# Denominator rows broadcast from 32 source rows instead of 8, with a new instruction order and one relu free to choose its engine

## The chip, the cores and the metric

The kernel runs on one core of one Trainium2 chip. The time is the device time of a run in microseconds (us). Each version is run several times and the runs in the fast state are compared. All comparisons use fast runs alone; two slow runs of the kernel before (552.36 and 390.58 us) are left out of them. TensorE's clock was granted in full (0.998 to 1.000) in every trace that this text reads. The experiments ran in four groups (1 to 4, 5 to 8, 9 to 11, and 12) on four chips, each beside the kernel before, whose medians there were 268.31, 268.89, 268.65 and 269.29 us; so a ratio is compared first with those of its own group.

## The reference, cut to what matters

Four layers follow one another over x of 1 x 2048 x 512 bf16 values: linear attention with 32 heads of 16 columns, a feed-forward block of 1376 hidden units, and both once more with the same weights.

```python
def _A_ref(x, wqkv, wo):                     # attention without softmax
    ...                                      # q, k, v by head
    phi = lambda t: jnp.where(t > 0, t + 1, jnp.exp(t)) + 1e-6
    pq, pk = phi(q), phi(k)
    kv  = jnp.einsum("bhsd,bhse->bhde", pk, v)
    z   = jnp.einsum("bhsd->bhd", pk)
    num = jnp.einsum("bhqd,bhde->bhqe", pq, kv)
    den = jnp.einsum("bhqd,bhd->bhq", pq, z)[..., None] + 1e-6
    o = num / den                            # one denominator per head and row
    return o.transpose(0, 2, 1, 3).reshape(B, S, D) @ wo

def _B_ref(x, w1, w2):
    return jnp.maximum(x @ w1, 0) @ w2       # written with einsum there

x = x + _A_ref(_layernorm(x), A_wqkv, A_wo)
x = x + _B_ref(_layernorm(x), B_w1, B_w2)
... # the same two lines once more
```

## The kernel before

Every operation is put on a list with what it reads and writes. Two text tables then fix the whole schedule: ORDER gives the place of each operation in the instruction streams and, for those that may run on either engine, a letter (`a` ScalarE, `d` VectorE); BANKS gives the PSUM bank of each tile. Both come from an offline search.

The denominators of a chunk of 512 rows go this way: a matmul with the mask Zc, logarithm and exponential on ScalarE (which makes 1/den), a write to DRAM, and four broadcasts that bring each head's row to the 16 partitions of that head. VectorE then multiplies.

```python
mm_group(... Zc[:, j, :] ..., name="den%d" % t)     # 32 columns per group of 8 heads: 4 copies of each head
g.add(ACT, ... ACTF.Ln ...)
g.add(ACT, ... ACTF.Exp, scale=-1.0 ...)            # rsp = 1/den
r = rdram[cur_layer[0] // 2, t]
dma(lambda e: e.dma_start(r, rsp[:, s, :]), ...)
for j in range(4):
    i = 4 * t + j
    dma(lambda e, i=i, j=j: e.dma_start(xn[:, i, :],
            r[32 * j:32 * j + 8, :].unsqueeze(1).broadcast_to([8, 16, 512])), ...)   # 8 rows, each 16 times
...
# a_den_mul: VectorE, L855
e.tensor_tensor(unit_ap(us[j]), unit_ap(us[j]), xn[:, i, :], ALU.mult)
```

After an attention block the residual is added, the row is centred into `xn`, and one DMA transposes two row tiles of `xn` into `Tb`, from which the next matmuls read. It is issued from the same queue as the broadcasts.

```python
# resid_a
g.add_flex([(ACT, ... activation(xn[:, i, :], xres[:, i, :], ACTF.Identity, bias=nmf ...)),
            (DVE, ... tensor_scalar(xn[:, i, :], xres[:, i, :], nmf ..., ALU.add))], ..., name="cen%d" % i)
# tr_dma, L484
dma(lambda e: e.dma_start_transpose(Tb[:, lo:hi, ...], xn[:, lo:hi, ...]), ...)
```

The feed-forward block uses products of seven multiplications for eight. Its fourth output block is summed by `hadd` and gets its relu from `hq`, on VectorE only:

```python
g.add(DVE, ... tensor_tensor(out_ap(1, 1), pv(X), s6 ..., ALU.add), name="hadd%d_%d" % (t, js[0]))
g.add(DVE, ... tensor_scalar(out_ap(1, 1), out_ap(1, 1), 0.0, None, ALU.max), name="hq%d_%d" % (t, js[0]))
```

Two groups of matmuls do no work and keep TensorE busy at the start; some experiments change their number:

```python
for ... in range(WARM): last = e.matmul(psv[:, wt, :], wrm[:, 0:128], wrm[:, :], ...)           # WARM = 10
... [(psv[:, wt, :], wrm[:, 0:128], wrm[:, :], True, True, False)] * NFILL                      # NFILL = 2
```

## Time and profile before

| | before |
|---|---|
| time, median of 3 runs | 268.69 us (the two fast ones are 268.33 and 268.69) |
| span in the profile | 267.4 us |
| TensorE busy | 260.0 us |
| VectorE busy | 240.7 us |
| ScalarE busy | 202.4 us |
| TensorE stalls between head and tail | about 2.6 us as the prediction counts them (2.4 corrected, see the end) |

The table is read from the bottom up. An engine that is 97% busy leaves little to gain, and the last line says how much: it is the sum of the gaps between matmuls, worked out with its lines in the prediction below.

### The profile page before, as it was taken

To read this page: it belongs to the slowest core of one execution; us is meant where nothing else is said; L and a number is where in the kernel's file an instruction comes from. 1 tells how busy PE (TensorE), PEld (TensorE's weight loads), DVE (VectorE), ACT (ScalarE), POOL (GpSimd) and SP (SyncE) were. 2 spreads that over 40 slices of the span, in tenths; PEclk is the share of its full clock that TensorE was granted. 3 is DMA by queue.
4 is the path that set the end of the run, shared out by engine and by line. 5 is a ranking of instruction groups with operands and counts; after the bars stand their busy time and mean duration, and the time that the engine had idled before them with its cause. 6 is when DMAs were issued, how large, how long until landed. Compare 5 with 4: busy or idle time off the path is not lost.

```text
span 267.4 us, 5269 instructions
## 1 busy us (share of the span) xinstructions
PE 260.0 (97%) x1919; PEld 171.5 (64%) x1937; DVE 240.7 (90%) x660; ACT 202.4 (76%) x446; POOL 19.6 (7%) x30
## 2 busy tenths in 40 slices
PE   7999999998999999999999999999999999999995
PEld 2444444546447888887875654454786778888883
DVE  4999999999789999999998998499989999889975
ACT  3999965889888786487788998799999869745320
POOL 4021000000030002201011000000000000130000
PEclk9999999999999999999999999999999999999999
DMA  6954882346234061401403400322592245201104
GB/s 209 382 115 82 195 306 71 127 78 162 38 107 91 0 81 21 82 0 22 77 13 69 78 2 2 103 93 43 131 175 50 39 42 99 81 0 22 80 2 157
DMA packets 47626, 23.61 MB, mean 88 GB/s; under 512 B 37008, under 2 KB 46192, under 8 KB 47600
## 3 DMA queue, kind: packets, MB, share of 16 engines
q1 hardware_dynamic: 47456, 23.24, 35.3%
q8 instruction: 15, 0.25, 0.4%
q14 instruction: 11, 0.09, 0.1%
q10 hardware_dynamic: 144, 0.03, 0.1%
HBM read 11.21 MB, written 3.15 MB: 54 GB/s over the span
## 4 chain that ended last, share of the span: by engine, by line
PE 85%; DVE 7%; DMA 5%; issue 1%; ACT 1%; SPq 0%; DVEq 0%
PE ps L538 84%; DMA Tb<-xn 3%; DMA xin<-in_A_x_dram 1%; DVE xres L551 1%; DVE xres L582 1%; DVE ps L1035 1%; DVE xn L970 1%; DVE xin L1061 1%; DVE xn L558 0%; ACT big L518 0%; PE ps L501 0%; DVE xn L578 0%; DVE bst L445 0%; DVE KVT L649 0%; ACT xn L556 0%
## 5 line engine op out<-in xcount | busy, mean ns | idle before, releaser
L520 ACT ACTIVATE escr<-ps 128x512 bf16<-128x512 f32 x56 | 33.3, 614 | 7.1 <-PE ps L538 7.0
L1021 ACT ACTIVATE big<-ps 128x512 bf16<-128x512 f32 (+1 forms) x57 | 29.2, 530 | 8.0 <-PE ps L538 7.7
L545 ACT ACTIVATE sqscr<-xres 128x512 bf16<-128x512 f32 x48 | 30.4, 633 | 5.3 <-DVE xres L582 2.6
L518 ACT ACTIVATE big<-ps 128x512 bf16<-128x512 f32 x56 | 33.3, 611 | 1.4 <-PE ps L538 1.3
L538 PE MATMUL ps<-big,xn 128*128 128x512 bf16 x122 | 30.2, 379 | 0.3
L538 PE MATMUL ps<-Tb,wqkv 128*128 128x512 bf16 x128 | 30.5, 379 | 0.0
L538 PE MATMUL ps<-gw,big 128*128 128x512 bf16 x121 | 29.2, 379 | 0.3
L538 PE MATMUL ps<-wqkv,Tb 128*128 128x512 bf16 x92 | 22.7, 379 | 0.7 <-ACT Tb L508 0.3
L524 DVE TENSOR_TENSOR big<-big,escr 128x512 bf16<-128x512 bf16 x56 | 22.4, 420 | 0.8 <-ACT big L518 0.2
L538 PE MATMUL ps<-w2s,big 128*128 128x256 f16 x160 | 21.9, 272 | 0.1
L538 PE MATMUL ps<-xn,w 128*128 128x256 f16 x140 | 21.8, 273 | 0.0
L538 PE MATMUL ps<-xn,xin 128*128 128x256 f16 x140 | 21.4, 273 | 0.2 <-DVE xn L970 0.2
L538 PE MATMUL ps<-w,big 128*128 128x256 f16 (+3 forms) x114 | 21.6, 301 | 0.0
L538 PEld LDWEIGHTS ps<-Tb,wqkv 128*128 128x128 bf16 x128 | 12.2, 98 | 14.3 <-issue 0.2
L538 PE MATMUL ps<-Tb,wper 128*128 128x256 bf16 x140 | 21.3, 272 | 0.0
L538 PEld LDWEIGHTS ps<-gw,big 128*128 128x128 bf16 x128 | 12.4, 98 | 12.7 <-issue 0.5
L538 PEld LDWEIGHTS ps<-big,xn 128*128 128x128 bf16 x128 | 12.0, 97 | 13.1 <-issue 0.7
L571 POOL TENSOR_TENSOR rstdf<-varf,nhalf 128x4 f32<-128x4 f32 x8 | 9.6, 1201 | 145.1 <-DVE varf L569 145.1
L538 PE MATMUL ps<-w,xin 128*128 128x256 bf16 (+2 forms) x145 | 19.7, 269 | 0.1
L1004 ACT ACTIVATE ps<-ps 128x512 f32<-128x512 f32 (+1 forms) x32 | 16.5, 514 | 4.4 <-PE ps L538 2.4
L1104 ACT ACTIVATE ps<-ps 128x256 f32<-128x256 f32 x27 | 10.0, 371 | 11.8 <-PE ps L538 10.3
L522 DVE TENSOR_SCALAR escr<-escr 128x512 bf16<-128x512 bf16 x56 | 15.6, 288 | 2.4 <-ACT escr L520 2.4
(160 smaller groups left out, 544.8 us busy)
## 6 DMA issues: line engine op xcount, KB each, us to landing
xn<-rdram SPq DMA_DIRECT2D x32, 128.0 KB
wqkv<-in_A_wqkv_dram SPq DMA_DIRECT2D x3, 512.0 KB, 7.1
xin<-in_A_x_dram SPq DMA_DIRECT2D x3, 512.0 KB, 7.9
out_dram<-xn SPq DMA_DIRECT2D x3, 512.0 KB, 2.6
w<-in_B_w_dram SPq DMA_DIRECT2D x1, 1376.0 KB, 6.9
w<-in_B_w_dram SPq DMA_DIRECT2D x1, 1280.0 KB, 9.9
rdram<-rsp SPq DMA_DIRECT2D x8, 128.0 KB, 1.7
wo<-in_A_wo_dram SPq DMA_DIRECT2D x1, 512.0 KB, 10.1
```

Of the source, the lines that this page charges most:

```text
L518: g.add(ACT, lambda e: e.activation(dst_ap, psv[:, b, :], ACTF.Identity, bias=1.0 + 1e-6, scale=1.0), [("ps", b)], [dst_key], C_ACT_PSUM, ...
L520: g.add(ACT, lambda e: e.activation(escr[:, s, :], psv[:, b, :], ACTF.Exp), [("ps", b)], [("escr", s)], C_ACT_EXP, name=name + "_exp")
L522: g.add(DVE, lambda e: e.tensor_scalar(escr[:, s, :], escr[:, s, :], 1.0, 1e-6, ALU.min, ALU.add), [("escr", s)], [("escr", s)], C_DVE_BF4 ...
L524: g.add(DVE, lambda e: e.tensor_tensor(dst_ap, dst_ap, escr[:, s, :], ALU.max), [dst_key, ("escr", s)], [dst_key], 340.0, name=name + "_phi")
L538: last = e.matmul(o, l, r, start=st, stop=sp, skip_group_check=skip)
L545: g.add(ACT, lambda e: e.activation(sqscr[:, q, :], xres[:, i, :], ACTF.Square, accum_out=dst[:, i:i + 1]), [("xres", i)], [("sqscr", q), ...
L551: g.add(DVE, lambda e: e.scalar_tensor_tensor(xres[:, i, :], psv[:, b, :], 0.0, src, ALU.add, ALU.add, accum_out=s1f[:, i:i + 1]), [("ps", ...
L571: g.add(POOL, lambda e: e.tensor_tensor(rstdf[:, sl], varf[:, sl], nhalf[:, 0:4], ALU.pow), [("varf", t), ("nhalf",)], [("rstdf", t)], C_P ...
L582: g.add(DVE, lambda e: e.scalar_tensor_tensor(xres[:, i, :], psv[:, b, :], rstdf[:, i:i + 1], xres[:, i, :], ALU.mult, ALU.add, accum_out= ...
L1004: g.add_flex([(ACT, lambda e: e.activation(dst(), psv[:, src, 0:W], ACTF.Identity), cost(C_ACT_PSUM)), (DVE, lambda e: e.tensor_copy(dst() ...
L1021: g.add_flex([(ACT, lambda e: e.activation(out_ap(r, m), pv(b), ACTF.Relu), cost(C_ACT_PSUM)), (DVE, lambda e: e.tensor_scalar(out_ap(r, m ...
L1104: g.add_flex([(ACT, lambda e: e.activation(psv[:, c1, cols], psv[:, c2, L], ACTF.Identity), 290.0), (DVE, lambda e: e.tensor_copy(psv[:, c ...
```

## The change

The intent: a broadcast that reads 32 rows can be spread over all 16 DMA rings, one that reads 8 only over 8 (a ring is here the share of a transfer that one of the core's 16 DMA engines moves; each reports its end by a semaphore update of its own); a relu that may run on either engine relieves VectorE; and with these new costs the order is searched again.

```diff
-ORDER, BANKS   (old tables; 63 and 3 lines)
+ORDER, BANKS   (new tables; 11 operations go from ScalarE to VectorE, 8 the other way, about 100 matmul groups move)
-        esel, ehead = ...                      # never read
-        def den_consts(): ...                  # filled them
-   affine_select(zm1[:], onesf[:, 0:32], [[0, 4], [-16, 8]], ...)
+   affine_select(zm1[:], onesf[:, 0:32], [[-16, 8], [0, 4]], ...)
-   affine_select(zmask[:], zm1[:], [[0, 4], [16, 8]], ...)
+   affine_select(zmask[:], zm1[:], [[16, 8], [0, 4]], ...)
-   dma_start(xn[:, i, :], r[32 * j:32 * j + 8, :].unsqueeze(1).broadcast_to([8, 16, 512]))     # cost 650
+   dma_start(xn[:, i, :], r[32 * j:32 * j + 32, :].unsqueeze(1).broadcast_to([32, 4, 512]))    # cost 550
-   g.add(DVE, tensor_scalar(... ALU.max), name="hq...")
+   g.add_flex([(DVE, tensor_scalar(... ALU.max)), (ACT, activation(... ACTF.Relu))], name="hq...")
```

The mask edit puts the four copies of a head side by side, so that 32 consecutive rows each read 4 times give the same 128 rows as 8 rows each read 16 times. One of the moves is of the centring of row tile 2 in the first attention block (`cen2`), from ScalarE to VectorE.

> **What bounds the kernel now.** I read the engine totals first, then the chain that ended last, then who waited for whom, and only then the queues.
>
> ```profile
> PE 260.0 (97%) x1919; PEld 171.5 (64%) x1937; DVE 240.7 (90%) x660; ACT 202.4 (76%) x446; POOL 19.6 (7%) x30
> ...
> PE 85%; DVE 7%; DMA 5%; issue 1%; ACT 1%; SPq 0%; DVEq 0%
> PE ps L538 84%; DMA Tb<-xn 3%; DMA xin<-in_A_x_dram 1%; DVE xres L551 1%; DVE xres L582 1%; DVE ps L1035 1%; DVE xn L970 1%; DVE xin L1061 1%; DVE xn L558 0%; ACT big L518 0%; PE ps L501 0%; DVE xn L578 0%; DVE bst L445 0%; DVE KVT L649 0%;
> ```
>
> TensorE is the bound: busy 97%, 85% of the chain, clock 1.0 throughout. The change's title speaks of a full VectorE (90%), but a full VectorE costs time only where a matmul waits for it. Busy is not proof, since matmul ends are modelled, so I also took the start-to-start distances of the 1919 matmuls: the median is 216 ns for 512 columns and 109 ns for 256, and nearly all sit on the median. Some 16 gaps are one matmul too long with no waiter; those are missing records (1937 weight loads against 1919 matmuls), not stalls.
>
> The idle 7.4 us (267.4 - 260.0) splits into 1.24 before the first matmul, about 3.1 after the last (it starts at 264.25), and 3.2 of gaps, of which 0.8 belongs to the first layer norm, before 9 us. Of the rest one gap stands out. The chain in order of time shows it, and later stretches without a break:
>
> ```profile
> 61.63 4.97 DMA Tb<-xn
> 66.60 0.05 issue
> 66.65 7.31 PE ps L538 x38
> ...
> 194.44 4.37 DMA Tb<-xn
> 198.81 0.03 issue
> 198.83 0.43 DVE xn L970
> 199.27 0.05 issue
> 199.32 4.42 PE ps L538 x48
> ...
> 217.80 46.18 PE ps L538 x426
> ```
>
> At 66.65 TensorE waits for a transpose (L484) of 4.97 us; in the last feed-forward block it then works 46 us without an entry for anything else. The list of waits agrees:
>
> ```profile
> PE ps L538 <- DMA Tb<-xn: 1.0, 1, 1.0
> ...
> DVE xn L970 <- DMA Tb<-xn: 0.9, 1, 0.9
> ```
>
> Counted as start-to-start excess, the avoidable stalls after the head are 1.21 us at 66.65, 0.36 at 199.32, 0.31 at 176.56 (the KVT step), 0.31 at 102.97 and about 0.4 of crumbs: **2.6 us in all, 1.0% of the run**. No rescheduling that leaves the matmuls alone can win more between the head and the tail.
>
> **What the Trainium skill says.** "DMA: Bandwidth & Descriptors", section "Why a DMA increments its semaphore by 16 and not by 1": a transfer uses the largest k up to 16 that divides the slowest dimension of both sides, and the sequencer posts 16 - k at once. The old broadcast has 8 source rows, hence k = 8. The trace agrees: all 32 broadcasts show 9 semaphore updates (one early jump, then 8), everything else 16, and the page therefore gives no landing time for them:
>
> ```profile
> xn<-rdram SPq DMA_DIRECT2D x32, 128.0 KB
> ...
> Tb<-xn SPq DMA_TRANSPOSE x30, 3.2
> ...
> big<-hrt SPq DMA_TRANSPOSE x8, 2.5
> ```
>
> "TensorE: Matmul & The Clock Gate", "Wait — 56ns, not 53.3ns?", gives N/2.4 GHz plus about 2.5 ns for a warm matmul, 215.7 ns for 512 columns; the trace has 216, so these matmuls cannot run closer. "ScalarE: Activation LUTs", "What ACT_TABLE_LOAD costs", gives 186 ns + 0.833 ns per column for an ACTIVATE with immediate operands: 613 and 399 ns for 512 and 256 columns. The trace has 596 and 387 for L1021, the same relu out of PSUM.
>
> **The change, part by part.**
>
> *Broadcasts.* The columns of the denominator are reordered so that each head's four copies are adjacent; a broadcast then reads 32 rows 4 times instead of 8 rows 16 times. Bytes stay 128 KB, in 128 packets of 1 KB of 46 ns each (median of the trace). Per ring that is 16 x 46 = 0.74 us now and 8 x 46 = 0.37 us afterwards. The queue issues one every 0.62 us (0.58 plus a gap), so today a group of four gains a backlog of about 0.12 us per transfer, and afterwards none. From the semaphores a broadcast takes 2.6 to 2.8 us from issue to landing when alone and first, 3.1 to 3.4 at the end of a group, 3.7 to 4.4 behind a transpose. I estimate 2.3 us afterwards for each: rows arrive 0.4 us earlier at the front of a group, 0.9 us at its end. But the multiplication that consumes them (L855, 32 x 418 ns) shows no wait at all today, so this gain is hidden. What remains is what queues behind: the transpose at 194.44 (4.37 us, normally 3.1) and the hidden-unit transposes at 65.48 (3.7) and 198.25 (4.2), normally 2.4. The first gates the 0.36 us stall at 199.32. Its gain is up to 0.3 us, less because the new order puts one broadcast (0.6 us of issue) ahead of that transpose.
>
> *The 66.65 stall is not the broadcasts'.* The late transpose lands on 15 of 16 rings by 65.06 and on the last at 66.60. A 16 KB instruction fetch occupies one ring from 64.51 to 65.43, an 8 KB one from 65.15. At 140.13 there is the same picture with no broadcast near: fetch at 142.87, 15 rings at 143.30, the last at 144.93. So wider broadcasts do not cure it; a shifted schedule may move the transpose off the fetch, or another transpose onto one. I give it about even odds: 0.6 us expected of 1.2.
>
> *relu of the fourth block.* I compared the order texts: only 4 of 21 go to ScalarE, all in the last block, three of 256 columns and one of 512. VectorE loses 3 x 0.220 + 0.285 = 0.95 us, ScalarE gains 3 x 0.40 + 0.61 = 1.8 us. This lies in 204 to 264 us, where ScalarE is the emptier engine and TensorE has an unbroken 46 us: worth next to nothing.
>
> *Dead constants.* ehead and esel (0.199 + 0.220 us of VectorE near 41 and 44 us) go. TensorE is not waiting there: under 0.1 us.
>
> *The new order.* Eleven flexible evacuations move from ScalarE to VectorE and eight the other way, with some hundred matmul groups reordered, mostly in the last block. VectorE's total should stay within 1 us of 240.7. TensorE's work is identical.
>
> Sum: -0.6 (fetch collision, even odds), -0.2 (199), -0.2 for the smaller stalls that a new search should have tidied, -0.1 (constants), +0.2 for stalls that a new order makes: **-0.9 us, 268.69 to 267.8 us**.
>
> **The rivals.** (1) *Broadcasts are the bottleneck of the attention blocks*, and earlier rows pull everything forward by about 1 us per group. For it: the two long transposes in the chain stand next to broadcast groups. Against: no wait at L855, and the fetch explains the larger. It would give about 266.5, still capped by the 2.6 us. (2) *VectorE is the real bound*, as the title says, and relief of it pays. For it: 90% busy, and most small TensorE waits name VectorE. Against: those add up to little over 1 us, and the other moves hand VectorE more than half of the relief back. At most 1 us. (3) *The new order is worse on the chip than in the search that made it*: one tile needed too early stalls TensorE by 0.5 to 2 us, or a transpose meets an instruction fetch at a tight spot; with reordered groups in every block, 269 to 270 is possible.
>
> **Range and chances.** The floor is 268.7 - 2.6 = 266.1; two undisturbed runs of before differ by 0.36 us. So 266.5 to 269.3. Faster by 2% needs 263.3, below that floor; slower by 2% needs 274.1, that is 5 us of new stalls. Within 2%: 97%.
>
> **What would show it.** The broadcasts get a landing time on the page, near 2.3 us; TensorE's busy time stays within 2 us of 260; VectorE's within 1 us of 240.7; the hidden-unit transposes behind broadcasts fall to 2.4 to 3 us; the wait for a transpose near 66 us goes or stays with the instruction fetch's timing and not with the broadcasts. I would be wrong if TensorE had stalls that its records hide, if the spread of the rings slowed the transposes (all 16 rings shared, where 8 were free), or if the head or tail moved: their 9 and 3 us are outside my 2.6.

## The result, and the profile after

The kernel after takes 266.88 us (median of 4 runs, 266.66 to 267.25) against 268.85 us (median of 4 runs of the kernel before, the two of the table and the slow one among them). The ratio is 0.9935, with a 95% interval of 0.9914 to 0.9956: 0.65% faster, or 1.75 us (the fast runs' means are 268.67 and 266.92), which counts as the same at 2%. A ratio here is the record's, of the fast runs of the same rounds; it lies near the ratio of the means and is not quite that of the medians. A later set of six runs gave 0.9938 (0.9924 to 0.9951).

The profile page of the kernel after, engine totals, the chain that ended last by engine, and the landing time of the broadcasts (count, size of one, median us from issue to landing):

```profile
PE 258.9 (98%) x1919; PEld 172.3 (65%) x1937; DVE 240.3 (91%) x657; ACT 202.0 (76%) x447; POOL 18.7 (7%) x30
...
PE 92%; DVE 3%; DMA 2%; issue 1%; SPq 0%; DVEq 0%
...
xn<-rdram SPq DMA_DIRECT2D x32, 128.0 KB, 2.6
```

The busy times of all engines moved by about 1 us or less. What fell is the chain's share of other things than matmuls: TensorE's is 92% instead of 85%, and the transposes' 3% is gone from it. The broadcasts have a landing time now, 2.6 us, where the page had none.

The chain of waits of the kernel after, in order of time (start us, length us, what), around the place where the kernel before lost most, and in the last block:

```profile
54.89 17.90 PE ps L536 x124
72.79 0.05 issue
72.84 7.54 PE ps L536 x51
80.39 0.05 issue
...
185.65 0.16 issue
185.81 14.61 PE ps L536 x145
...
215.36 46.33 PE ps L536 x426
```

L536 is the matmul line, L538 before. From 54.89 to 72.79 us TensorE runs without a break, straight through the place where the transpose of 4.97 us stood; and from 185.81 to 200.42 through the one where that of 4.37 us stood. The list of waits (engine, what it wrote and its line, what it waited for: us in all, times, longest) has no entry of TensorE for a transpose any more; these are its largest entry for transposes (the other, L960, is 0.2 us) and the one for broadcast rows:

```profile
DVE big L702 <- DMA Tb<-xn: 1.2, 2, 0.8
...
DVE big L845 <- DMA xn<-rdram: 0.4, 1, 0.4
```

L845 is the multiplication that was L855. It had no wait before and has one now, of 0.4 us.

To place the gain, I cut the TensorE work at two matmuls that both kernels have: the third denominator of the first attention block (start at 56.47 us before) and the first of the second block (165.94 us), and compared start times. The head up to 56 us became shorter by 0.35 us, the first half by 1.49 and the second half, up to the last matmul, by 0.45: together 2.29, the difference of the spans 267.4 and 265.1. Over all versions measured below the head scatters from -0.5 to +0.2 us, once +1.84, with no link to the edits that I could find; so I count it as scatter and explain the other two.

**First half.** 1.21 us are the stall at 66.65, and 0.31 the one at 102.97; both are gone. **Second half.** 0.36 us are the stall at 199.32, gone too.

What happened at 66 us is read from the semaphore updates of the one transpose, which come ring by ring. In the kernel before: issued at 61.63, fifteen rings done at 65.06, the sixteenth at 66.60 (latency 4.97). After: 60.89, 64.07, 64.30 (3.40). In both an instruction fetch of TensorE's program, one packet of 16 KB, falls into this time: 64.51 to 65.43 before, 63.60 to 64.53 after. The DMA view of the kernel after, 61 to 68 us, has it (q8: packets, MB, share) beside the transpose that landed in time (median us to landing); experiment 9 shows the same view of the kernel before:

```profile
q8 instruction: 1, 0.02, 0.8%
...
Tb<-xn SPq DMA_TRANSPOSE x1, 3.4
```

The prediction put the late ring down to that fetch, and gave even odds that a new order would avoid it. The experiments had to decide between the fetch and the broadcasts.

### The profile page after: what moved, and what is told of

Same layout as the page of the kernel before. It is cut to its first block, busy times and chain, and to the rows that moved or that the text cites. A ratio compares the mean times of both kernels' runs of the same rounds, so it can differ in the third digit from the quotient of the medians.

```text
span 265.1 us, 5275 instructions
## 1 busy us (share of the span) xinstructions
PE 258.9 (98%) x1919; PEld 172.3 (65%) x1937; DVE 240.3 (91%) x657; ACT 202.0 (76%) x447; POOL 18.7 (7%) x30
## 3 DMA queue, kind: packets, MB, share of 16 engines
HBM read 11.21 MB, written 3.15 MB: 54 GB/s over the span
## 4 chain that ended last, share of the span: by engine, by line
PE 92%; DVE 3%; DMA 2%; issue 1%; SPq 0%; DVEq 0%
PE ps L536 92%; DMA wqkv<-in_A_wqkv_dram 2%; DVE bst L443 1%; DVE big L522 0%; DVE escr L520 0%; DVE xn L475 0%; DVE xn L576 0%; DVE Tb L507 0%; SPq L379 0%; SPq L381 0%; DVE KVT L647 0%; DVE xn L1166 0%; DVE mv L444 0%; DVEq L1389 0%; PE ps L499 0%
## 5 line engine op out<-in xcount | busy, mean ns | idle before, releaser
L536 PE MATMUL ps<-Tb,wqkv 128*128 128x512 bf16 x128 | 30.8, 379 | 0.0
L536 PE MATMUL ps<-big,xn 128*128 128x512 bf16 x122 | 30.1, 379 | 0.3
L536 PE MATMUL ps<-gw,big 128*128 128x512 bf16 x121 | 29.2, 379 | 0.5 <-issue 0.2
L536 PE MATMUL ps<-wqkv,Tb 128*128 128x512 bf16 x92 | 22.5, 379 | 1.0 <-DMA wqkv<-in_A_wqkv_dram 0.5
L536 PE MATMUL ps<-w2s,big 128*128 128x256 f16 x160 | 21.7, 273 | 0.0
L536 PE MATMUL ps<-xn,w 128*128 128x256 f16 x140 | 21.7, 273 | 0.0
L536 PE MATMUL ps<-xn,xin 128*128 128x256 f16 x140 | 21.5, 273 | 0.0
L536 PE MATMUL ps<-w,big 128*128 128x256 f16 (+2 forms) x114 | 21.4, 301 | 0.0
L536 PEld LDWEIGHTS ps<-Tb,wqkv 128*128 128x128 bf16 x128 | 12.1, 98 | 14.0 <-issue 0.2
L536 PE MATMUL ps<-Tb,wper 128*128 128x256 bf16 x140 | 20.8, 273 | 0.0
L536 PEld LDWEIGHTS ps<-gw,big 128*128 128x128 bf16 x128 | 12.3, 98 | 12.5 <-issue 0.5
L536 PEld LDWEIGHTS ps<-big,xn 128*128 128x128 bf16 x128 | 12.0, 98 | 13.0 <-issue 0.7
L536 PE MATMUL ps<-w,xin 128*128 128x256 bf16 (+2 forms) x145 | 19.6, 269 | 0.0
L569 POOL TENSOR_TENSOR rstdf<-varf,nhalf 128x4 f32<-128x4 f32 x8 | 8.5, 1065 | 143.5 <-DVE varf L567 143.5
L536 PEld LDWEIGHTS ps<-w2s,big 128*128 128x128 bf16 x160 | 15.2, 98 | 3.7 <-DVE xres L1090 0.9
```

The costliest lines, as they stand in the source:

```text
L536: last = e.matmul(o, l, r, start=st, stop=sp, skip_group_check=skip)
L569: g.add(POOL, lambda e: e.tensor_tensor(rstdf[:, sl], varf[:, sl], nhalf[:, 0:4], ALU.pow), [("varf", t), ("nhalf",)], [("rstdf", t)], C_P ...
```

## The experiments

**Theory A** (that of the prediction): the stall at 66 us belongs to the fetch, the new order moved the transpose to where the fetch doesn't hold it, and the broadcasts are worth about 0.2 us elsewhere. **Rival B:** the wide broadcasts free the queue, and the order is nothing but their consequence. **Rival C:** VectorE is the bound, and the relus on ScalarE are what paid.

### 1. Wide broadcasts alone, in the old order

```diff
 # the kernel before, with the two mask lines and
-   r[32 * j:32 * j + 8, :].unsqueeze(1).broadcast_to([8, 16, 512])
+   r[32 * j:32 * j + 32, :].unsqueeze(1).broadcast_to([32, 4, 512])
```

> The kernel before with the wide broadcasts alone (mask columns reordered, 32 rows read 4 times), its own order and relus. My theory (the broadcasts are hidden, the stall near 66 us comes from an instruction fetch on one ring): ratio 0.997 to 1.000, the broadcasts land in about 2.4 us, the stall near 66.6 us is still there with over 0.8 us, only the 0.36 us near 199 us shrinks. Rival 1 (the broadcasts delay the transposes): the stall near 66 us goes, ratio 0.993 to 0.995, the whole gain.

Measured: 268.61 us against 268.31, ratio 1.0004 (0.9987 to 1.0020): nothing. The chain of this kernel at the same place:

```profile
61.41 0.36 ACT big L518
61.77 4.95 DMA Tb<-xn
66.72 0.05 issue
66.76 7.31 PE ps L538 x38
```

The transpose is as late as before (its last ring at 66.72, the other fifteen at 65.19), with wide broadcasts in place: the stall is 1.20 us. So rival B falls for this stall. The second half is 0.45 us shorter than before, though, exactly what the kernel after has; the transpose near 194 us fell from 4.37 to under 3.5 us. This part is the broadcasts' own. Why the unprofiled runs do not show these 0.45 us isn't settled; the interval reaches to 0.9987, that is 0.35 us.

### 2. The new order with the old broadcasts

```diff
 # the kernel after, with the two old mask lines and
-   r[32 * j:32 * j + 32, :].unsqueeze(1).broadcast_to([32, 4, 512])
+   r[32 * j:32 * j + 8, :].unsqueeze(1).broadcast_to([8, 16, 512])
```

> The changed kernel with the old narrow broadcasts (8 rows read 16 times, old mask), the new order and the four relus on ScalarE kept. My theory (the order makes the gain): ratio 0.992 to 0.995 to the kernel before, no transpose stall near 65 us, a wait of up to 0.4 us may come back near 197 us. Rival 1: 0.997 to 1.000, stall back.

Measured: 269.25 us, ratio 1.0034 (1.0015 to 1.0052). This is slower than before, and a clear miss: theory A had the order carry most of the gain, and expected 0.992 to 0.995. The list of waits, and the chain near 66 us, of this kernel:

```profile
DVE big L845 <- DMA xn<-rdram: 3.6, 5, 1.8
```

```profile
63.69 4.39 DMA xn<-rdram
68.08 0.02 issue
68.10 0.04 DVE big L845
68.14 0.31 issue
68.44 0.69 DVE ps L995
```

VectorE now waits 5 times, 3.6 us in all, for broadcast rows, where the kernel before has no such wait and the kernel after one of 0.4 us. The search had been told that a broadcast costs 550 instead of 650 and placed the multiplications earlier. The transpose is issued at 61.75 instead of 60.89, and here all its rings are late (66.39), so that TensorE stalls there for 0.91 us again; and the second half, where the kernel after gains 0.45 us, loses 0.69. In the second half the rows are the cause that the trace shows: VectorE waits 0.30 and 0.84 us for them near 179 and 180 us, with no fetch on their broadcasts, and TensorE then waits for VectorE (0.74 us at 187.93). At 66 us the trace does not show this: no broadcast was queued ahead of that transpose, and a fetch (64.04 to 64.97) fell on it and on the broadcasts behind it, so broadcasts and fetch are not separated there. So order and broadcasts cannot be added up: the new order needs the rows early, in the second half at least.

### 3. The new order with all relus of the fourth block on VectorE

```diff
 # the kernel after, four entries of ORDER
-1301a ... 1427a ... 1443a ... 1533a
+1301d ... 1427d ... 1443d ... 1533d
```

> The changed kernel with the four relus of the fourth block back on VectorE. My theory (TensorE works unbroken there): equal to the changed kernel, ratio 0.9925 to 0.9950 to the kernel before, no new stall of over 0.2 us after 205 us. Rival 2 (VectorE is the bound there): 0.5 us or more is lost, ratio over 0.996.

Measured: 266.74 us, ratio 0.9939 (0.9924 to 0.9954), the same as the kernel after. The busy times of 56 us of the last block (stretch, length, then TensorE, weight loads, VectorE, ScalarE and GpSimd with their instruction counts, clock, DMA share, GB/s), first of the kernel after, then of this one:

```profile
204.00:260.00 56.00, 55.89 (x495) 45.95 (x495) 50.85 (x118) 33.37 (x77) 3.99 (x4) 1.00 0.18 48
```

```profile
204.00:260.00 56.00, 55.90 (x494) 45.90 (x495) 51.38 (x122) 31.88 (x73) 4.00 (x4) 1.00 0.18 48
```

VectorE has four instructions more and TensorE is as full as it was. Even here, where the relus are, VectorE is no bound: rival C falls.

### 4. The instruction fetch moved, first try

TensorE's program has 3,888 instructions, and one fetch packet appears for about every 256 of them. More instructions early therefore bring a later fetch forward in time. Here the idle matmuls at the start are cut into more and narrower ones, with about the same number of columns in all (10 x 512 = 5,120 and 31 x 165 = 5,115); with the weight loads that is 42 instructions more.

```diff
 # the kernel before
-WARM=10 ... e.matmul(psv[:, wt, :],     wrm[:, 0:128], wrm[:, :], ...)
+WARM=31 ... e.matmul(psv[:, wt, 0:165], wrm[:, 0:128], wrm[:, 0:165], ...)
```

> The kernel before with 31 warm-up matmuls of 165 columns in place of 10 of 512: the same warm-up time, 42 more TensorE instructions, so each of TensorE's instruction fetches comes some 42 instructions (about 4 us near 60 us) earlier. Nothing else differs. My theory: the fetch moves from 64.5 to about 60.6 us, the transpose issued at 61.6 us lands by 65.2 instead of 66.6 us, the 1.2 us stall goes, ratio 0.995 to 0.996. If the broadcasts make the stall, it stays and the ratio is 1.000.

Measured: 268.75 us, ratio 1.0015 (0.9992 to 1.0039). The fetch moved from 64.51 to 60.46 us and the transpose's latency fell from 4.97 to 3.45 us, as theory A has it; but the fetch now lay on the issue of the transpose before it, which took 2.15 us instead of 1.25 and held up this one (issued at 62.16). Stall 0.60 us, and 0.47 at 198.35 where the kernel before has 0.36. For theory A in the trace, but not clean, and a miss in the time (0.995 to 0.996 was expected).

### 5 and 6. The new order in one half only

The new ORDER and BANKS are used up to entry 700 and the old ones behind it, and the other way round; the entries 575 to 840, counted from 0, are the same in both orders (old numbers adjusted for the two constants that went), so the cut falls where nothing differs. Both have the wide broadcasts.

```diff
 # 5: ORDER = new[:700] + old[700:], BANKS likewise      # 6: ORDER = old[:700] + new[700:]
```

> The changed kernel with the new order (and its PSUM banks) up to the middle of the run and the old order after it, wide broadcasts throughout, the four relus on VectorE. My theory: two thirds or more of the gain lies in the first half, where the transpose that TensorE waits for near 66 us is issued earlier: ratio 0.9945 to 0.996, no stall near 66 us. If the gain lies in the last block, 1.000.

> The mirror: old order up to the middle, new order after it, wide broadcasts throughout. My theory: the stall near 66.7 us is there with about 1.2 us, ratio 0.998 to 1.000. If the last block makes the gain, 0.994.

Measured: 267.00 us, 0.9930 (0.9914 to 0.9947), for the new first half, and 268.24 us, 0.9974 (0.9958 to 0.9990), for the new second half. The first half's order, with the wide broadcasts, is enough for the gain of the kernel after; the second half's is not. Both are a little faster than expected. In the trace of the first, however, the stall was still there with 0.75 us (in that of the second with 1.19): this one profiled run met the fetch. Its time equals that of the kernel after; whether the unprofiled runs escaped the fetch can't be seen, since only a profiled run leaves a trace.

### 7. One single move: the centring of row tile 2

In the new order `cen2` runs on VectorE. It feeds the transpose in question, so this one letter might explain the whole first half.

```diff
 # experiment 1, one entry of ORDER
-353a
+353d
```

> The kernel before with wide broadcasts and one more edit: the centring of row tile 2 of the first attention block on VectorE in place of ScalarE (one letter of the order text). My theory: the transpose that needs it is issued 0.3 to 0.5 us earlier and gets out of the way of the instruction fetch: the stall near 66 us falls under 0.3 us, ratio 0.995 to 0.996 (0.9955). If that move is not what matters, the stall stays at 1.2 us and the ratio at 1.000.

Measured: 267.85 us, ratio 0.9963 (0.9946 to 0.9980). The stall is 0.81 us, not the under 0.3 that was expected, since the transpose still took 4.76 us; the stall of 0.31 us at 102.97 went. The kernel of experiment 6 ran in the same rounds and has the same broadcasts and the old order in its first half: against it the means of the times differ by 0.33 us (267.88 and 268.21). The trace shows 0.37 us in the first half against experiment 1, and not by escaping the fetch.

### 8. The fetch moved by waits that are already met (failed)

```diff
 # the kernel before: ahead of 140 matmuls of the first projections
+    e.wait_ge(sem_eng[DVE], 1)
```

> The kernel before with 140 more waits for a semaphore that is already satisfied, between matmuls of the first 40 us, so that TensorE's instruction fetches come 140 instructions earlier: the one at 64.5 us should come between 50 and 57 us, away from the transpose issued at 61.6 us. Nothing else differs. My theory: this transpose lands 3.1 to 3.3 us after its issue in place of 4.97, the stall near 66.6 us falls under 0.2 us; ratio about 0.9955 if the waits cost nothing and no other fetch hits a tight transpose. If the broadcasts make the stall, it stays.

Measured: 268.93 us, ratio 1.0005 (0.9983 to 1.0026). The fetch stayed where it was (64.56), with a stall of 1.23 us. The waits did not become instructions: the trace has 3,888 instructions of TensorE as before, and 470 of them instead of 330 carry a wait. The run says nothing on the theory, but as a second look at the old order it shows two things. At 66 us all 16 rings were late here (66.57 to 66.81), not one. And the second half was 0.72 us longer than in the trace before: the transpose at 194.71, behind four narrow broadcasts and with no fetch until its last 0.05 us, took 5.08 us.

### 9. The fetch moved far enough

```diff
 # the kernel before, with the edit of experiment 4 and
-NFILL=2  ... [(psv[:, wt, :],   wrm[:, 0:128], wrm[:, :],   ...)] * NFILL
+NFILL=30 ... [(psv[:, wt, 0:8], wrm[:, 0:128], wrm[:, 0:8], ...)] * NFILL
```

That is 2 x (21 + 28) = 98 instructions more, ahead of all real work.

> The kernel before with 31 warm-up matmuls of 165 columns for 10 of 512, and 30 fill matmuls of 8 columns for 2 of 512 in a gap of the first layer norm: about the same time, 98 more TensorE instructions ahead of everything. (Of the two earlier tries, one moved the fetch onto the issue of the transpose before, the other did not move it.) My theory: the fetch of 64.5 us comes at 55 to 60 us, the transpose issued near 61.6 us lands after 3.0 to 3.3 us, and the stall near 66 us (1.20) falls under 0.2 us. Ratio 0.995 to 0.997 if no other fetch takes its place. If the broadcasts make the stall, it stays at 1.2 us.

Measured: 268.27 us against 268.65, ratio 0.9984 (0.9965 to 1.0002). The fetch moved from 64.51 to 54.23 us. The DMA view of 61 to 68 us, the queues (packets, MB, share) and the transposes with their median us to landing, of the kernel before and of this one:

```profile
q8 instruction: 1, 0.02, 0.8%
...
Tb<-xn SPq DMA_TRANSPOSE x2, 4.1
```

```profile
q14 instruction: 1, 0.01, 0.5%
...
Tb<-xn SPq DMA_TRANSPOSE x2, 3.1
```

And the chain of this kernel at that place:

```profile
9.76 82.80 PE ps L538 x521
```

TensorE runs 82.80 us without a break, from 9.76 to 92.56, in the old order and with the old, narrow broadcasts. The transpose took 3.05 us, and the first half is 1.30 us shorter. This settles the cause of the 1.21 us: the fetch. (q8 carries TensorE's instructions; q14's packet is another, half as large, and is there in both.) The total gained only 0.4 us, with an interval that reaches no gain, short of the 0.995 to 0.997 that was expected. All later fetches moved too: one at 193.88 fell on the transpose issued at 192.74 (4.55 us), which cost 0.55 us at 197.80 (0.36 at 199.32 before), and the second half is 0.19 us longer. That leaves most of the difference unexplained: the profiled run (267.59 us) was the fastest of its six, and the others left no trace.

### 10. The same on the kernel after

> The changed kernel with the same 98 extra instructions. If the fetch near 63.6 us still costs the changed kernel something in some executions (the mixed kernel with its first half had a stall of 0.75 us from it), this is faster than the changed kernel by up to 0.5 us: ratio 0.9915 to 0.9935 to the kernel before. If it has left the fetch behind in all of them: equal to it within 0.001.

Measured: 267.62 us, ratio 0.9964 (0.9947 to 0.9980): slower than the kernel after (0.9938 in the same rounds, experiment 11), a miss. At 66 us there was nothing left to win, and a transpose late at 198.10 now cost 0.83 us, with 0.25 us at 46.78 and 80.86.

### 11. The kernel after again

> The changed kernel itself, on the same chip and in the same rounds as the two others, and a second trace of it: ratio 0.993 to 0.995; the transpose of the first attention block near 61 us lands within 3.5 us of its issue, or, if its profile of before was a lucky one, after 4.8 us with a stall of about 0.75 us.

Measured: 266.98 us, ratio 0.9938 (0.9924 to 0.9951). The transpose took 3.05 us and TensorE did not stall, as in the first trace of this kernel and in that of experiment 3.

### 12. Old order, wide broadcasts, fetch moved by 114 instructions

```diff
 # experiment 9 with the wide broadcasts and
-NFILL=30
+NFILL=38
```

> The kernel before in its old order, with the wide broadcasts and with 114 extra TensorE instructions in the head (as in the last run, 8 fills more, so that the fetch near 193 us comes earlier than the transpose there). If the gain of the change is the escape from the fetch (1.2 to 1.5 us) plus the lighter queue of the second attention block (0.45 us), and not the order as such, this old order reaches the changed kernel: ratio 0.992 to 0.9945, no stall over 0.4 us at 60 to 70 us or at 190 to 205 us. If the new order is needed: 0.996 or more although both stalls are gone. If a fetch meets another tight transpose, the trace shows that stall, and the ratio is that much higher.

Measured: 268.22 us against 269.29, ratio 0.9961 (0.9929 to 0.9994), short of the 0.9945 hoped for at worst. The stall at 66 us is gone, but a fetch at 195.25 met the transpose issued at 195.13 (4.37 us; stall 0.36), and the profiled run was also the slowest of its six, with 1.84 us more in the head. No version that I made beats the kernel after clear of the noise; experiments 3 and 5 equal it.

### What the traces show together

The first half, as change of TensorE's start times against the kernel before:

| | narrow broadcasts | wide broadcasts |
|---|---|---|
| old order | 0 | -0.08 us |
| new order | -0.19 us | -1.49, -1.38 (again), -1.41 us (relus on VectorE) |
| old order, fetch moved | -1.30 us | -1.15 us |

Over all 14 traces I took the latency of every transpose into `Tb` issued after 50 us. Of 222 that met neither a fetch (16 KB of q8 or 8 KB of q14) nor a broadcast queued ahead of them, none took over 3.36 us (median about 3.15). Of 93 that a fetch overlapped, 42 took over 3.6, the longest 4.98. Seven behind narrow broadcasts took 3.08 to 5.08 us, ten behind wide ones 3.18 to 3.53; the few with both a fetch and broadcasts are left out.

Which of them are held up depends on when the fetch begins. Taking TensorE's 16 KB fetches alone, and again no broadcast ahead:

| the fetch began | transposes | latency |
|---|---|---|
| 0.16 to 0.92 us before the issue of the transpose | 18 | 3.02 to 3.33 us |
| 0.48 to 2.91 us after it | 48 | 42 took 3.61 to 4.98, three 3.44 to 3.45, three 3.05, 3.05 and 3.40 us |
| 3.01 to 3.26 us after it | 4 | 3.04 to 3.27 us |

The 42 landed 0.97 to 1.95 us after the end of the fetch. Only 13 of them had one late ring with the other fifteen done over 0.5 us before; in 29, that of experiment 8 among them, more rings or all were late. The 8 KB packets alone held none up: 24 transposes, none over 3.46 us.

What stays open is the escape itself. The three at 3.05, 3.05 and 3.40 us are those at 61 us in the kernel after (twice) and in experiment 3, with the fetch 2.46, 2.53 and 2.71 us after the issue. Elsewhere transposes with the fetch 2.68 and 2.71 us after their issue took 4.74 and 4.55 to 4.84 us (between 2.30 and 2.68 there are no others to compare), and the same transpose in experiment 5, where the order is the same up to there, took 4.85 us with the fetch at 2.80. So the distance in time alone does not explain why the new order escapes, and the records do not say which ring a packet used. That the stall at 66 us in the old order was the fetch's is shown by experiment 9; why a fetch in the same place costs the kernel after nothing is not shown.

## Why the prediction was right, and where it was not

The prediction said 267.8 us (266.5 to 269.3) and 97% for within 2%. The result is 266.88: in the range and within 2%, with twice the gain that was named, 1.75 instead of 0.9 us.

- **The bound and the cap of 2.6 us** held. TensorE's busy time stayed within 2 us of 260 (258.9) and VectorE's within 1 us of 240.7 (240.3), as named. The profile's gain outside the head is 1.94 us.
- **The broadcasts' landing** was estimated at 2.3 us; the median is 2.55 (2.22 to 4.61), against 3.17 of the narrow ones (2.62 to 4.37). That the gain is hidden was right in the old order (experiment 1).
- **"The 66.65 stall is not the broadcasts'"** was right, and experiment 9 shows it. The term was mis-sized: 0.6 us, as even odds of 1.2, where the three full traces of the new order with wide broadcasts (one of them with the relus on VectorE) lost the whole 1.2; experiment 5, with half of that order, lost 0.46. This is the largest part of the missing gain, and since the escape is not explained, it has to be called luck: the even odds fell well.
- **The stall at 199** was put at -0.2 us. The second half gained 0.44 to 0.45 us in every version with wide broadcasts and unshifted fetches, whatever the order. The rest of the missing gain is here, as far as the traces go; the times of experiment 1 do not show it.
- **The smaller stalls**, -0.2 in the sum: the one at 102.97 went, 0.31 us. The one at 176.56 was misread: two weight loads (176.33 and 176.35) stand before one matmul there, so 0.22 of its 0.31 us is a missing record, and the cap is 2.4 and not 2.6 us. In experiment 11, where the record is there, the gap is 0.09 us. (The 3.1 us after the last matmul were likewise counted from its start; from its end they are 2.9.)
- **The relus on ScalarE: "worth next to nothing"** was right: 0.9939 without and 0.9935 with them.
- **The step that failed** is that the sum treats its parts as independent. Each part was costed against the old timing, but the new order is slower than the old (1.0034) without the wide broadcasts. The slack at the multiplication was no fixed property: the new order used it up (waits of 3.6 us with the narrow broadcasts, 0.4 with the wide ones, none before). How much of the loss in its first half is the fetch's and how much the rows' stays open.
- **"The hidden-unit transposes behind broadcasts fall to 2.4 to 3 us"** did not come: the three in the trace of the kernel after took 3.63, 5.29 and 4.00 us, the last two with a 16 KB fetch (197.56 to 199.03) on them. The reading of before had missed the fetch at 199.47 on its own example at 198.25. In the old order with wide broadcasts the one near 66 us did fall, to 2.71 us (experiment 1).
- Of the **rivals**, the first (broadcasts as the bottleneck) falls in the old order by experiment 1 and comes true in the second half of the new order with narrow ones (experiment 2); the second (VectorE) falls by experiment 3; the third (a worse order) came true only without the wide broadcasts.

## What to carry to other kernels

Look at a late transfer ring by ring: one ring that comes late while fifteen are done asks for another cause than a loaded queue, and a move of the suspected cause by itself (here some dozens of idle instructions early on) decides it. The reverse does not hold: most transposes that a fetch held up were late on more than one ring, so all rings late does not clear the fetch. In a schedule tuned to the last per cent, a part's worth depends on the others: the broadcasts alone gave nothing, the order alone lost 0.34%, and together they won 0.65%. Gains of this size can hang on where an instruction fetch falls, so repeat the trace before giving an edit the credit.

## What the Trainium skill lacked or had wrong

- "Runtime: NRT & Kernel Launch", section "Instruction fetch mechanics", says that the instruction memory is refilled in blocks of 16 KiB, 256 instructions, over a DMA queue of the sequencer's own, and calls the cost of crossing a block "mostly hidden". The traces agree on the size: 15 packets of 16 KB for 3,888 instructions of TensorE. It lacks that a fetch goes along with delays of the kernel's own transfers: of 48 transposes with a fetch that began 0.48 to 2.91 us after their issue 42 took over 3.6 us, up to 4.98, and none of the 222 free of fetches and broadcasts took over 3.36; one delay made TensorE stall for 1.21 us.
- "DMA: Bandwidth & Descriptors", section "Why a DMA increments its semaphore by 16 and not by 1", gives the rule by which 8 rows use 8 rings and 32 rows 16, and the traces agree (9 and 16 semaphore updates). It lacks what that costs: 3.17 against 2.55 us to the landing of 128 KB, and 3.08 to 5.08 against 3.18 to 3.53 us for a transpose queued behind (seven and ten cases).
- Nothing that the pages state was found wrong.
